# The 48 T sums of the gate and up stage made by GpSimd instead of VectorE

## The chip, the core and the metric

The kernel runs on one core of one Trainium2 chip. The metric is the device time of one execution, in microseconds (us). A core has a TensorE (PE in the profile), a VectorE (DVE), a ScalarE (ACT), a GpSimd (POOL) and a SyncE (SP). Each works through its own instructions in order and waits on semaphores for the others. SyncE and GpSimd also issue the DMA transfers.

## The reference

With x of 2048 tokens by 640, the kernel computes a gated mix of a Fourier layer and a feed-forward layer, all in float32:

```python
g = _sigmoid((x * gate_w).sum(-1, keepdims=True))
a = einsum("ts,bse->bte", seq_re, x @ hid_re.T) - einsum("ts,bse->bte", seq_im, x @ hid_im.T)
b = (_gelu(x @ w_gate) * (x @ w_up)) @ w_down      # 640 -> 1728 -> 640
return g * a + (1 - g) * b
```

The change lies in the middle of `b`: in the inner values `_gelu(x @ w_gate) * (x @ w_up)` and in what is prepared from them for the product with `w_down`.

## The kernel before, in words

**Products.** Every float32 operand is split into a high part (ACT, line 82) and a low part (DVE, line 85: raw minus high), and a product is three matmuls (`mm3`, lines 101 to 103). On top of that the products are made in blocks of two by two with sums of blocks (Strassen and Winograd), so that seven products stand for eight. The sums of blocks of a right operand are called T here, those of the weights S.

**Stages.** In the profiled execution a first stage (to about 54 us) prepares the tokens and makes block 0 of the 1728 inner columns. The gate and up stage (about 54 to 340 us) is the loop over `f` = 1 to 12 at line 1182, 128 inner columns each. After it come the product with `w_down` (loop over `kseq`, line 1269), and then the two Fourier products.

**Inner values.** For each `f` and each half of the tokens, `tp` = 0 or 1, the generator `gate_up` makes two tiles of 128x512, `s2` and `s1` (gelu of the gate times the up product; lines 556, 561 and 563). `keep` (line 398) stores each to DRAM in `hA` by a DMA issued from GpSimd. Two neighbouring `f` make a pair `k`. Per pair and `tp` four T sums of inner values are stored in `hT`: one at the end of the odd `f` (line 566), three after the even `f` (`last_sums`, lines 573 and 575, and `last_sum`, line 579). That is 6 pairs x 2 x 4 = 48 sums. Some of these tiles are reused soon: the buffer `s5` that holds the sums of lines 566 and 575 is one of those that the next blocks take again, as are the buffers of `s2` and `s1`.

**Products across the halves.** In odd blocks from `f` = 3 on, `together` and `together_up` make products whose right operand is a sum over the two token halves, T1 to T3. These three do not fit in on-chip memory all the time: for `f` = 5, 7, 9 and 11 they are loaded again from DRAM by `load_across` (line 1153), 512 KB each, issued from GpSimd: `xq` for `together` late in the even block ahead, `xu` for `together_up` inside the odd block (line 1249). `together_up` needs T1 first, in the product into `pZ..u`.

**What sets the order.** Inside the loop the order of PE, ACT, DVE and GpSimd is the order of the Python code (`in_order`, line 1181). The steps of `gate_up`, `together` and `together_up` follow each other as the loops at lines 1238 to 1248 say. Between them `fill` (line 1158) takes side work from the list `fills`: weight sums and splits for the next block, `make_up` (the S sums and splits of `together_up`'s weights, whose high part is `wu3h` and so on), and the T sums of the pair before, which come from `todo` at line 1187. Each piece has a cost in units that the author chose; `fill` goes on while the cost done is under 1.25 times the share of PE work done, but it ends its turn before a piece of cost 0 once it has done one (line 1162). In blocks 5, 7, 9 and 11 the T sums come first in the list; in block 3 they follow the sums over the halves.

Of the kernel before, what the change touches and what calls it, by code (L numbers as in the profile page):

```python
# [12 lines left out]
ALU = mybir.AluOpType  # L13
# [24 lines left out]
def kernel(  # L38
# [27 lines left out]
    nc = tc.nc  # L66
# [8 lines left out]
    def mtile(dt, name):  # L75
        return pool.tile([P, T], dt, tag="m", name=name, bufs=14)

    def bank(name):
        return psum.tile([P, T], F32, tag="ps", name=name, bufs=8)
# [19 lines left out]
    def mm3(ps, lhs, rhs, first, last):  # L99
        (lh, ll), (rh, rl) = lhs, rhs  # L100
        nc.tensor.matmul(ps, lh, rh, start=first, stop=False, skip_group_check=True)  # L101
        nc.tensor.matmul(ps, lh, rl, start=False, stop=False, skip_group_check=True)  # L102
        nc.tensor.matmul(ps, ll, rh, start=False, stop=last, skip_group_check=True)  # L103
# [32 lines left out]
    def pair(dt, name):  # L136
        return slot(dt, [P, 2, T], name)
# [4 lines left out]
    def at(hilo, i):  # L142
        h, l = hilo
        return h[:, i], l[:, i]

    def copy(src, name):
        m = mtile(F32, name)
        nc.scalar.activation(m, src, AF.Copy)  # L148
        return m

    tt = nc.vector.tensor_tensor
# [53 lines left out]
    def pair_of(f):  # L205


        return 0 if f < PAIRED or f >= NF else 2 - (f - PAIRED + 1) % 2
# [188 lines left out]
    def keep(to, i, src):  # L397
        nc.gpsimd.dma_start(to[:, i], src)  # L398
# [21 lines left out]
    hid, todo = {}, deque()  # L420
# [74 lines left out]
    def gate_up(f, W, B, tp, s5, s1t, xs, s4):  # L495

        n = f"{f}_{tp}"  # L500
        kind = pair_of(f)
        X, Z = bank(f"pX{n}"), bank(f"pZ{n}")
        xs[tp] = X
        x1, x2 = at(B[5], 0), at(B[5], 1)
        k, second = divmod(f - 1, 2)

        def prod(ps, a, b, first):
            for i in range(2):
                mm3(ps, W[a, i], at(B[b], i), first and i == 0, True)

        prod(X, "A11", (1, 1), True)
        yield 136
        if not kind:
            V = bank(f"pV{n}")
            nc.scalar.activation(V, X, AF.Copy)
        else:
            s1 = s1t[kind - 1, tp] if (kind, tp) != (1, 1) else None
            if s1 is not None:
                tt(s1, s1, X, op=ALU.add)
        yield  # L520
        if not kind:
            prod(V, "A12", (2, 1), False)
            mm3(V, W["g5"], x1, False, True)
            yield 204
            s1 = mtile(F32, f"s1{n}")
            nc.scalar.activation(s1, V, AF.Gelu_apprx_tanh)
            yield
        prod(Z, "S1", "T1", True)
        mm3(Z, W["u5"], x2, False, True)
        yield 204  # L530
        nc.scalar.activation(s5, Z, AF.Copy)
        yield
        prod(X, "S2", "T2", False)
        yield 136
        s2 = copy(X, f"s2{n}")
        yield
        mm3(Z, W["D"], x2, False, False)
        yield 68
        if kind:
            s1 = s1t[kind - 1, tp]  # L540
            nc.scalar.activation(s1, s1, AF.Gelu_apprx_tanh)
        yield
        prod(X, "S3", "T3", False)
        yield 136
        tt(s5, s5, X, op=ALU.add)  # L545
        yield
        prod(Z, "S4", (2, 2), False)
        yield 136
        tt(s2, s2, Z, op=ALU.add)  # L549
        nc.scalar.activation(s2, s2, AF.Gelu_apprx_tanh)  # L550
        yield
        if not kind:
            prod(X, "A22", "T4", False)
        mm3(X, W["u5"], x1, False, True)
        yield 68 if kind else 204
        tt(s2, s2, s5, op=ALU.mult)  # L556
        keep(hA[tp][k], 1 + 2 * second, s2)
        if kind:
            c21 = s4[kind - 1, tp]
            tt(c21, c21, X, op=ALU.add)  # L560
            tt(s1, s1, c21, op=ALU.mult)
        else:
            tt(s1, s1, X, op=ALU.mult)
        keep(hA[tp][k], 2 * second, s1)
        if not second:
            tt(s5, s2, s1, op=ALU.subtract)
            keep(hT[tp][k], 0, s5)
            hid[tp] = s2, s5
            yield
        h12, t1 = hid.pop(tp)  # L570

        def last_sums():
            tt(h12, s2, h12, op=ALU.subtract)  # L573
            keep(hT[tp][k], 2, h12)
            tt(t1, s2, t1, op=ALU.subtract)
            keep(hT[tp][k], 1, t1)

        def last_sum():
            tt(s5, s1, t1, op=ALU.subtract)
            keep(hT[tp][k], 3, s5)  # L580

        todo.extend([(122, last_sums), (61, last_sum)])
        yield

    def sums_left(engine, a11, a12, a22, a21, to):
# [595 lines left out]
    with in_order(PE, ACT, DVE, POOL):  # L1181
        for f in range(1, NF):
# [41 lines left out]
            s5 = pair(F32, f"s5{f}")  # L1224
            xs = {}
            work = [gate_up(f, W, Bs[tp], tp, s5[:, tp], s1t, xs, s4) for tp in range(2)]
            more = together(f, W, Tp, s1t, xs) if kind == 1 else iter(())
            more_up = together_up(f, W, up, s4) if kind == 1 else iter(())
# [124 lines left out]
    for i, (j, ri, b, sp) in enumerate(cseq):  # L1353
# [65 lines left out]
        else:  # L1419
# [21 lines left out]
            if lst:  # L1441
                for d in range(2):
                    s2 = copy(X[d], f"s2{n}{d}")
# [10 lines left out]
                for d in range(2):  # L1454
                    s2, a, r, c12 = sv["s2", d], sv["a", d], sv["r", d], sv["c12", d]
# [41 lines left out]
    for i, (tp, b, p) in enumerate(useq[: 3 * ND]):  # L1497
# [43 lines left out]
        for q in range(2):  # L1541
            s2, a = es[q]
            tt(a, s2, Q[q], op=ALU.add)
        for q in range(2):
            s2, a = es[q]
# [47 lines left out]
    for q in range(2):  # L1593
        tail(X[q], ("A11", q, True), 0)
        sv["x", q] = copy(X[q], f"yx{q}")
        s2, c21, c22 = es[q]
# [105 lines left out]
```

## Time and profile before

| | |
|---|---|
| three timed runs | 1020.31, 1021.18 (median), 1022.54 us |
| span of the profiled execution, first to last instruction | 1019.2 us |
| timed runs above that span | 1.1 to 3.3 us, the median 2.0 us |
| busy, whole span | PE 1014.9, DVE 826.7, ACT 485.1, POOL 163.2 us |
| busy from 54 to 340 us (gate and up) | PE 286.00, DVE 228.05, ACT 135.48, POOL 73.67 us |
| granted TensorE clock | 1.000 |

No time of the profiled execution is listed apart from its span, so the span stands for it, and the 2.0 us to the median are what lies around it. A row of a view of groups reads: line, engine, operation, out<-in, shapes, count, then busy us and mean ns of one, then the idle time of the engine ahead of them and what ended it. A row of the timeline reads: start in us from the span's start, length in us, engine, line, operation, and in brackets the engine's idle time ahead of it and who ended it. A DMA row of POOL is the time in which GpSimd issues it; its landing is given apart. A matmul row lasts 0.39 us, but the next one starts about 0.23 us later.

### The profile page before, as it was taken

What the parts mean: (1) busy time and instruction counts of PE and PEld (TensorE: products, weight loads), DVE (VectorE), ACT (ScalarE), POOL (GpSimd) and SP (SyncE); (2) the same over time, 40 slices, a digit from 0 to 9 for tenths busy, and PEclk for the clock granted to TensorE, in tenths of its full rate; (3) what the DMA queues carried; (4) which work ended last, traced back from release to release, by engine and by line L of the source; (5) the groups of instructions that cost most, each with busy time, mean ns of one, the idle gap of its engine ahead of it and who ended that gap; (6) DMA issues with size and microseconds to landing.
All of it is one profiled execution on the core that took longest, in us unless ns stands there. A gap on an engine that the chain in (4) does not pass through costs nothing.

```text
span 1019.2 us, 13255 instructions
## 1 busy us (share of the span) xinstructions
PE 1014.9 (100%) x4483; PEld 840.1 (82%) x4483; DVE 826.7 (81%) x1158; ACT 485.1 (48%) x618; POOL 163.2 (16%) x291
## 2 busy tenths in 40 slices
PE   9999999999999999999999999999999999999998
PEld 7888888888888888888888888888888888888887
DVE  6987887977687979988887976898488859797796
ACT  5544535353535577557444443444344345455440
POOL 0122241323221200100001012102210200021121
PEclk9999999999999999999999999999999999999999
DMA  7468577968689999968874669658866877897855
GB/s 271 168 210 274 182 270 241 311 226 280 200 286 287 407 364 413 355 233 331 295 258 173 209 242 330 218 196 296 296 209 208 300 250 273 292 350 219 273 143 89
DMA packets 96068, 265.74 MB, mean 261 GB/s; under 512 B 12608, under 2 KB 26944, under 8 KB 96000
## 3 DMA queue, kind: packets, MB, share of 16 engines
q1 hardware_dynamic: 70512, 185.24, 52.9%
q0 software_dynamic: 25200, 79.46, 23.1%
q8 instruction: 35, 0.57, 0.2%
q14 instruction: 33, 0.27, 0.1%
q10 hardware_dynamic: 288, 0.20, 0.1%
HBM read 192.48 MB, written 70.27 MB: 258 GB/s over the span
## 4 chain that ended last, share of the span: by engine, by line
PE 100%; DVE 0%; issue 0%
PE pX L102 7%; PE pX L101 7%; PE pX L103 7%; PE pZ L101 5%; PE pZ L102 5%; PE pZ L103 5%; PE pL L103 3%; PE pL L101 3%; PE pL L102 3%; PE pV L103 2%; PE pV L101 2%; PE pV L102 2%; PE pR L103 1%; PE pY L103 1%; PE pQ L103 1%; PE pQ L101 1%
## 5 line engine op out<-in xcount | busy, mean ns | idle before, releaser
L82 ACT ACTIVATE ch<-csa 128x1024 fp32r<-128x1024 f32 x32 | 34.0, 1062 | 78.5 <-DVE csa L764 77.1
L85 DVE TENSOR_TENSOR cl<-cra,ch 128x1024 fp32r<-128x1024 f32 x32 | 39.1, 1222 | 27.0 <-ACT ch L82 24.9
L82 ACT ACTIVATE ch<-cra 128x1024 fp32r<-128x1024 f32 x32 | 33.9, 1059 | 52.3 <-DVE cl L85 16.3
L85 DVE TENSOR_TENSOR cl<-crb,ch 128x1024 fp32r<-128x1024 f32 x32 | 39.1, 1223 | 14.5 <-ACT ch L82 14.5
L103 PE MATMUL pL<-ch,xal 128*128 128x512 f32 x128 | 49.8, 389 | 0.0
L102 PE MATMUL pL<-cl,xah 128*128 128x512 f32 x128 | 49.8, 389 | 0.0
L101 PE MATMUL pL<-ch,xah 128*128 128x512 f32 x128 | 49.7, 389 | 0.0
L398 POOL DMA_DIRECT2D hA<-s x48 | 26.1, 544 | 138.1 <-DVE s L556 118.5
L82 ACT ACTIVATE ch<-crb 128x1024 fp32r<-128x1024 f32 x32 | 33.8, 1055 | 29.7 <-PE pL L102 11.6
L85 DVE TENSOR_TENSOR cl<-csb,ch 128x1024 fp32r<-128x1024 f32 x32 | 39.2, 1225 | 3.7 <-ACT ch L82 2.3
L85 DVE TENSOR_TENSOR cl<-csa,ch 128x1024 fp32r<-128x1024 f32 x32 | 39.1, 1221 | 2.1 <-ACT ch L82 1.1
L82 ACT ACTIVATE ch<-csb 128x1024 fp32r<-128x1024 f32 x32 | 34.0, 1062 | 11.7 <-DVE csb L767 5.0
L550 ACT ACTIVATE s<-s 128x512 f32<-128x512 f32 x24 | 15.2, 633 | 47.6 <-DVE s L549 47.6
L148 ACT ACTIVATE s<-pX 128x512 f32<-128x512 f32 x40 | 23.7, 596 | 29.0 <-PE pX L103 28.4
L82 ACT ACTIVATE kh<-kw 128x1024 fp32r<-128x1024 f32 x24 | 25.3, 1054 | 18.9 <-DMA kw<-wsd 14.5
L85 DVE TENSOR_TENSOR kl<-kw,kh 128x1024 fp32r<-128x1024 f32 x24 | 29.3, 1220 | 4.3 <-ACT kh L82 4.3
L545 DVE TENSOR_TENSOR s<-s,pX 128x512 f32<-128x512 f32 x24 | 16.4, 685 | 19.2 <-PE pX L103 19.1
L1349 POOL DMA_DIRECT2D uA<-c x8 | 4.3, 541 | 168.9 <-DVE c L1451 168.6
L398 POOL DMA_DIRECT2D hT<-s x48 | 26.0, 541 | 18.5 <-DVE s L573 8.1
L923 POOL DMA_DIRECT2D out<-ks x12 | 6.5, 541 | 137.4 <-DVE ks L922 136.5
L102 PEld LDWEIGHTS pL<-cl,xah 128*128 128x128 f32 x128 | 24.0, 188 | 5.0
L103 PEld LDWEIGHTS pL<-ch,xal 128*128 128x128 f32 x128 | 24.0, 188 | 5.0
(3626 smaller groups left out, 3479.0 us busy)
## 6 DMA issues: line engine op xcount, KB each, us to landing
cra<-in_ct SPq DMA_DIRECT2D x64, 512.0 KB, 4.2
crb<-in_ct SPq DMA_DIRECT2D x64, 512.0 KB, 5.0
hA<-s POOLq DMA_DIRECT2D x48, 256.0 KB, 5.7
hT<-s POOLq DMA_DIRECT2D x48, 256.0 KB, 5.0
kr<-hA SPq DMA_DIRECT2D x24, 512.0 KB, 7.7
kr<-hT SPq DMA_DIRECT2D x24, 512.0 KB, 7.3
ux<-uA SPq DMA_DIRECT2D x24, 512.0 KB, 6.2
ux<-uT SPq DMA_DIRECT2D x16, 512.0 KB, 7.3
```

What stands on the lines that cost most here:

```text
L82: nc.scalar.activation(hi, raw, AF.Copy)
L85: nc.vector.tensor_tensor(lo, raw, hi.bitcast(F32), op=ALU.subtract)
L101: nc.tensor.matmul(ps, lh, rh, start=first, stop=False, skip_group_check=True)
L102: nc.tensor.matmul(ps, lh, rl, start=False, stop=False, skip_group_check=True)
L103: nc.tensor.matmul(ps, ll, rh, start=False, stop=last, skip_group_check=True)
L148: nc.scalar.activation(m, src, AF.Copy)
L398: nc.gpsimd.dma_start(to[:, i], src)
L545: tt(s5, s5, X, op=ALU.add)
L550: nc.scalar.activation(s2, s2, AF.Gelu_apprx_tanh)
L923: nc.gpsimd.dma_start(acc4[:, t] if tp and e == 4 else out[2 * tp + t, e], src)
L1349: nc.gpsimd.dma_start(to[:, i], src)
```

## The change

Four `tt(...)`, which is `nc.vector.tensor_tensor`, become `nc.gpsimd.tensor_tensor`, and the costs that `fill` counts for the three late sums go from 122 and 61 to 0:

```diff
         if not second:
-            tt(s5, s2, s1, op=ALU.subtract)
+            nc.gpsimd.tensor_tensor(s5, s2, s1, op=ALU.subtract)
             keep(hT[tp][k], 0, s5)
...
         def last_sums():
-            tt(h12, s2, h12, op=ALU.subtract)
+            nc.gpsimd.tensor_tensor(h12, s2, h12, op=ALU.subtract)
             keep(hT[tp][k], 2, h12)
-            tt(t1, s2, t1, op=ALU.subtract)
+            nc.gpsimd.tensor_tensor(t1, s2, t1, op=ALU.subtract)
             keep(hT[tp][k], 1, t1)
 
         def last_sum():
-            tt(s5, s1, t1, op=ALU.subtract)
+            nc.gpsimd.tensor_tensor(s5, s1, t1, op=ALU.subtract)
             keep(hT[tp][k], 3, s5)
 
-        todo.extend([(122, last_sums), (61, last_sum)])
+        todo.extend([(0, last_sums), (0, last_sum)])
```

The instructions of GpSimd from the end of block 4 into block 5, before. `hA` and `hT` are the stores of inner values and of T sums, `xu` the loads of T1, T2 and T3 for `together_up`:

```order
L398 DMA hA_72<-s_1004 128x512
L398 DMA hT_78<-s_0_1122 128x512
L398 DMA hT_78<-s_985 128x512
L398 DMA hT_78<-s_1257 128x512
L398 DMA hT_84<-s_1_1136 128x512
L398 DMA hT_84<-s_985 128x512
L398 DMA hT_84<-s_1257 128x512
L1153 DMA xu_1485<-xv_562 128x1024
L1153 DMA xu_1527<-xv_563 128x1024
L1153 DMA xu_1529<-xv_564 128x1024
```

The same place on GpSimd in the change, from behind the last store of inner values to ahead of the first `xu` load:

```order
L573 TENSOR_TENSOR s_0_1112<-s_0_1321,s_0_1112 128x512
L398 DMA hT_78<-s_0_1112 128x512
L575 TENSOR_TENSOR s_985<-s_0_1321,s_985 128x512
L398 DMA hT_78<-s_985 128x512
L579 TENSOR_TENSOR s_1257<-s_1102,s_985 128x512
L398 DMA hT_78<-s_1257 128x512
L573 TENSOR_TENSOR s_1_1124<-s_1_1329,s_1_1124 128x512
L398 DMA hT_84<-s_1_1124 128x512
L575 TENSOR_TENSOR s_985<-s_1_1329,s_985 128x512
L398 DMA hT_84<-s_985 128x512
L579 TENSOR_TENSOR s_1257<-s_1004,s_985 128x512
L398 DMA hT_84<-s_1257 128x512
```

Between the last store of inner values and the first `xu` load stood six DMA issues; now six sums and six DMA issues stand there. The places in front of blocks 7, 9 and 11 are alike.

The instructions of ACT in block 3, before. `wu3h` is the high part of `together_up`'s weights, L468 the copy of `pH3u` into the bank `pV3u`, L148 are copies out of a bank:

```order
L148 ACTIVATE s_1110<-pH3t 128x512
L148 ACTIVATE s_0_1122<-pX_0_1026 128x512
L82 ACTIVATE wu3h<-wu3r 128x640
L148 ACTIVATE s_1_1136<-pX_1_1039 128x512
L468 ACTIVATE pV3u<-pH3u 128x512
L541 ACTIVATE s_1017<-s_1017 128x512
```

And in the change:

```order
L148 ACTIVATE s_1102<-pH3t 128x512
L148 ACTIVATE s_0_1112<-pX_0_1024 128x512
L148 ACTIVATE s_1_1124<-pX_1_1035 128x512
L468 ACTIVATE pV3u<-pH3u 128x512
L82 ACTIVATE wu3h<-wu3r 128x640
L541 ACTIVATE s_1017<-s_1017 128x512
```

The four pieces of cost 0 (two with two sums, two with one) take a turn of `fill` each, so the split of `wu3` comes two instructions later on ACT, behind L468. In blocks 5, 7 and 9 a split of a weight sum (`wa6` in block 5) comes earlier on ACT in the same way: it now stands ahead of the copies of `pH5t` and `pX` that come before L468.

The instructions of GpSimd at the end of block 1, before. `hA_65` and `hA_71` are the stores for the two halves of the tokens, `hT_77` and `hT_83` those of the first T sums, and `xp` stands for loads of block 2:

```order
L398 DMA hA_65<-s_0_651 128x512
L398 DMA hA_65<-s_0_606 128x512
L398 DMA hT_77<-s_565 128x512
L398 DMA hA_71<-s_1_664 128x512
L398 DMA hA_71<-s_1_619 128x512
L398 DMA hT_83<-s_565 128x512
L1138 DMA xp_559<-xp_790 128x512 x2
```

And in the change:

```order
L398 DMA hA_65<-s_0_651 128x512
L398 DMA hA_65<-s_0_606 128x512
L566 ISA
L566 TENSOR_TENSOR s_565<-s_0_651,s_0_606 128x512
L398 DMA hT_77<-s_565 128x512
L398 DMA hA_71<-s_1_664 128x512
L398 DMA hA_71<-s_1_619 128x512
L566 TENSOR_TENSOR s_565<-s_1_664,s_1_619 128x512
L398 DMA hT_83<-s_565 128x512
L1138 DMA xp_559<-xp_790 128x512 x2
```

Besides the two sums there is a new instruction, `L566 ISA`, which the build puts ahead of the first sum: it makes GpSimd load its instruction library. The first sum on GpSimd reads a buffer that the sum `xpt` at line 1122 of block 2 takes next on DVE, so that one now waits for GpSimd's sum; and on ACT the split of `xpt` (line 82) stands ahead of the copy at line 515 from bank `pX` into `pV`, on which PE goes on in block 2.

The order of PE does not change in the gate and up stage.

## The prediction

> **What bounds the kernel now.** The page of the profile comes first: its span, its busy shares, and the end of its chain of waits.
>
> ```profile
> span 1019.2 us, 13255 instructions
> PE 1014.9 (100%) x4483; PEld 840.1 (82%) x4483; DVE 826.7 (81%) x1158; ACT 485.1 (48%) x618; POOL 163.2 (16%) x291
> PE 100%; DVE 0%; issue 0%
> ```
>
> Then the view by windows for the gate and up stage (stretch, sum, then busy time of PE, PEld, DVE, ACT, POOL, then the granted clock), and the waits of PE over the whole span:
>
> ```profile
> 54.00:340.00 286.00, 286.00 (x1261) 236.36 (x1260) 228.05 (x414) 135.48 (x213) 73.67 (x133) 1.00 0.77 258
> PE idle L1017 <- PEq L1690: 0.8, 1, 0.8
> ```
>
> PE is busy for 286.00 of 286.00 us at full clock, and waits 0.8 us in all. DVE is busy 228.05 us there and gives up 48 sums, but nothing on PE waits for DVE, so this relief can bring no more than those 0.8 us. Conversely any operand that comes late adds its whole delay to the time, since PE has no pause that could take it up. So the question is which operands come late, and by how much. I went through the program of the change for what PE waits on, and set each against the time in this trace; three places matter.
>
> **What one sum costs.** On DVE the rows by groups are these; the last is the nearest to a slower reader:
>
> ```profile
> L566 DVE TENSOR_TENSOR s<-s,s 128x512 f32<-128x512 f32 x12 | 8.3, 692 | 0.4
> L575 DVE TENSOR_TENSOR s<-s,s 128x512 f32<-128x512 f32 x12 | 8.2, 684 | 0.0
> L85 DVE TENSOR_TENSOR ws6l<-ws6r,ws6h 128x1024 fp32r<-128x1024 f32 x1 | 1.2, 1220 | 0.0
> ```
>
> DVE loses 48 x 0.69 = 33 us, which is worth nothing. No row shows GpSimd computing. Call the duration of one sum on it g. The lower bound is 0.69 (as fast as DVE). The nearest row is 1.22, DVE over 1024 elements: the 512 of the one input and the 512 of the other, taken one after the other. To it I add the chance to meet DVE at the memory: DVE is busy (228.05 - 33) / 286 = 0.68 of the time, and half of its mean instruction there (228.05 / 414 = 0.55) is 0.27, so 0.68 x 0.27 = 0.19. I take g = 1.40 (an estimate), and as upper bound 1.22 + 0.69 = 1.91, where each sum waits for a whole DVE instruction.
>
> The Trainium skill, "GPSIMD Engine Reference", section "Elementwise — side-by-side cycle accounting", gives 4497 ns for a float32 addition over 2048 elements on GpSimd, 1.96 times DVE's, and keeps elementwise work on DVE; a quarter of it is 1.12 us (an estimate from that page). By it the sum below would be 4 x 1.83 + 1.2 + 4.3 = 12.8 instead of 19.8, and the time 1034.0. No trace here shows it yet.
>
> **Blocks 5, 7, 9 and 11: T1 comes late.** GpSimd's timeline in block 5, the same place in block 11, and PE's first use of T1 (tile `xu`) in both:
>
> ```profile
> 147.27 1.14 POOL L398 DMA_DIRECT2D hT<-s  x2
> 148.60 0.54 POOL L398 DMA_DIRECT2D hT<-s  x1 [0.19 <-issue]
> 152.13 0.55 POOL L1153 DMA_DIRECT2D xu<-xv  x1
> 290.31 1.14 POOL L398 DMA_DIRECT2D hT<-s  x2
> ```
>
> ```profile
> 161.26 0.40 PE L101 MATMUL pZ5u<-xu,wu5h 128*128 128x512 f32 x1
> 304.30 0.40 PE L101 MATMUL pZ11u<-xu,wu11h 128*128 128x512 f32 x1
> ```
>
> The landing of that first `xu` load after its issue, in blocks 7, 5 and 11:
>
> ```profile
> DMA to landing us min/median/max: 4.9/4.9/4.9
> DMA to landing us min/median/max: 5.3/5.3/5.3
> DMA to landing us min/median/max: 7.1/7.1/7.1
> ```
>
> From the place of the first `hT` store to PE's first use of T1 there are 161.26 - 147.27 = 13.99 us, in block 11 also 304.30 - 290.31 = 13.99. In the change the first sum starts there, and six sums with six stores stand ahead of the load. Two stores took 1.14, so 0.57 each; with 0.13 for the hand-over (under the 0.19 of "issue" in the second row) one sum and its store take g + 0.70. With the shortest landing, 4.9, since the stores now come less densely, T1 is late by 6 x (g + 0.70) + 4.9 - 13.99 = 3.51 us at g = 1.40. The four blocks are built alike: 4 x 3.51 = 14.0. At g = 1.22 it is 4 x 2.43 = 9.7, at 1.60 4 x 4.71 = 18.8. It is nothing up to g = 0.81. What hid the loads was the 9 us between issue at 152.13 and use; that cover is gone at g = 0.81.
>
> A second path runs beside it. On ACT the split of `wa6` now stands ahead of L468, and its input was computed by DVE into a buffer that a stored sum must leave first:
>
> ```profile
> DMA to landing us min/median/max: 3.9/3.9/3.9
> 159.21 0.62 ACT L82 ACTIVATE wa<-wa6r 128x512 fp32r<-128x512 f32 x1
> 160.83 0.58 ACT L468 ACTIVATE pV5u<-pH5u 128x512 f32<-128x512 f32 x1 [0.15 <-PE pH5u L103]
> 162.66 0.39 PE L101 MATMUL pV5u<-xT04h,wa5h 128*128 128x512 f32 x1
> ```
>
> The sixth store issues at 147.27 + 12.6 - 0.6 = 159.3 and lands 3.9 later, at 163.2; DVE, split, two copies and L468 follow, some 2.6 us in all, so `pV5u` is ready at 165.8. PE, late by 3.51, asks for it at 162.66 + 3.51 = 166.2. It lies beside the first delay and costs nothing more.
>
> **Block 3: a split behind L468.** ACT and PE there:
>
> ```profile
> 111.89 0.74 ACT L82 ACTIVATE wu3h<-wu3r 128x640 fp32r<-128x640 f32 x1 [0.31 <-DVE wu3r L249]
> 113.04 0.58 ACT L468 ACTIVATE pV3u<-pH3u 128x512 f32<-128x512 f32 x1
> 113.53 0.62 ACT L541 ACTIVATE s<-s 128x512 f32<-128x512 f32 x1
> 112.67 0.83 DVE L85 TENSOR_TENSOR wu3l<-wu3r,wu3h 128x640 fp32r<-128x640 f32 x1 [0.81 <-ACT wu3h L82]
> 113.53 0.40 PE L101 MATMUL pZ3u<-xv,wu3h 128*128 128x512 f32 x1
> 114.00 0.40 PE L103 MATMUL pZ3u<-xv,wu3l 128*128 128x512 f32 x1
> ```
>
> The split now starts where L541 did, at 113.53, and ends at 114.27, where PE wants `wu3h` at 113.53: about 0.8 late. The low part starts 0.78 after the split began (112.67 - 111.89) and takes 0.83, so it ends at 115.14, where PE wants it at 114.00: 1.14 late, of which the first 0.8 are the same delay. With the hand-over some 1.2 us in all, once. The sums do not enter here: it follows from the costs set to 0.
>
> **Block 2: the library.** The program of the change has `L566 ISA`, the load of GpSimd's library, ahead of the first sum:
>
> ```profile
> 69.83 0.54 POOL L398 DMA_DIRECT2D hA<-s  x1 [0.89 <-DVE s L563]
> 72.63 0.69 DVE L1122 TENSOR_TENSOR xpt<-xp,xp 128x512 f32<-128x512 f32 x1 [0.43 <-DMA hA<-s]
> 73.41 0.63 ACT L82 ACTIVATE xp<-xpt 128x512 fp32r<-128x512 f32 x1 [0.69 <-DVE xpt L1122]
> 73.94 0.58 ACT L515 ACTIVATE pV<-pX 128x512 f32<-128x512 f32 x1
> 75.34 0.39 PE L101 MATMUL pV<-x121h,wa2h 128*128 128x512 f32 x1
> ```
>
> DVE's L1122 now waits also for the first sum; behind it queue DVE's further sums and splits of `xp`, and on ACT the split of `xpt`, then L515, whose bank PE needs at 75.34. Let R be the load of the library. Load and sum start at 70.4 + 0.2 = 70.6; then come L1122 to the split's start (0.78), the split to L515 (0.53) and L515 to PE (0.6): PE is late by 70.6 + R + g + 1.91 - 75.34 = R + g - 2.83. No row shows R. From below it is 0 (a load that runs ahead of need); another engine's load of tables is the first row here, and transfers that GpSimd issues, the `xu` loads, the second:
>
> ```profile
> L690 ACT ACT_TABLE_LOAD x2 | 2.6, 1283 | 0.0
> DMA to landing us min/median/max: 3.4/6.0/7.5
> ```
>
> I take R = 6.0, the median of that second row, since code must come from DRAM by a transfer, too; the bounds are 0 and 7.5. That makes 6.0 + 1.4 - 2.83 = 4.6 us, once.
>
> The same page, section "Instruction dispatch", says that the first call of freshly loaded code pays about 5.95 us. By it this term would be 5.95 + 1.12 - 2.83 = 4.2.
>
> **The sum.** 14.0 + 1.2 + 4.6 = 19.8; the span becomes 1019.2 + 19.8 = 1039.0, and with the 2.0 us from span to median (1021.18 - 1019.2) 1041.0. The single sums of line 566 in later blocks have nothing tight behind them on GpSimd, and those of block 12 fall into the next stage; I cost both at nothing.
>
> **The rivals.** (1) *Sums that DVE blocks.* g = 1.91: each sum waits for a whole instruction of DVE. For it: DVE is still busy 68% of the time, with sums of two inputs. Then 4 x (6 x 2.61 + 4.9 - 13.99) = 26.3, plus 1.2, plus 6.0 + 1.91 - 2.83 = 5.1: 32.6, or 1053.8. Against it: a third of the time DVE is idle. The skill's "SBUF — State Buffer", section "Who interferes with whom", states this rule: a DVE instruction with two inputs in SBUF and a GpSimd one that reads SBUF exclude each other, and the second waits fully.
>
> (2) *Only what happens once.* g at 0.7 to 0.8, as on DVE: T1 is in time, and 1.2 + 6.0 + 0.7 - 2.83 = 5.1 remain: 1026.3. For it, the 692 ns row, and that GpSimd is busy only 73.67 of 286 us; against it, that nothing else suggests DVE's pace on this engine.
>
> (3) *Not slower.* The point that decides is g up to 0.81 together with R + g up to 2.83, a library loaded within 2 us (as in the ACT row, 1.28). Then all sums hide, only block 3's 1.2 us stays, and the time is 1022.4: no change.
>
> (4) *Faster.* It would need a wait of PE to remove, and the view of waits has 0.8 us of them.
>
> **How the numbers follow.** My forecast has 0.60, with a range of its own from g = 1.22 and R = 4 (9.7 + 1.2 + 2.4 = 13.3, 1034.5) to g = 1.60 and R = 7.5 (18.8 + 1.2 + 6.3 = 26.3, 1047.5). Rival 1 has 0.20, 2 has 0.10, 3 has 0.07 and 4 has 0.03. The range goes from 1027, just above rival 2, to 1056, which takes in rival 1 with R = 7.5 (34.1, 1055.3): 0.20 is left out, all of it below. A measurement of this kernel tells changes from about 0.2%, 2.0 us: faster 0.03, within 0.07, slower 0.90.
>
> **What would show it.** In the new profile PE should wait at `pZ5u`, `pZ7u`, `pZ9u` and `pZ11u` for the `xu` load, 3.5 us each; at `pV` of block 2 for ACT, 4.6 us; at `pZ3u` for `wu3h` and `wu3l`, 1.2 us together. Six pairs of sum and store should take 12.6 us on GpSimd. I am wrong if the rows of sums on GpSimd are under 0.81 or over 1.91 us, if the library shows no gap behind 70 us, or if PE waits at other places: for stores that must leave a buffer, or for DVE behind GpSimd.

## The result, and the profile after

| | before | after |
|---|---|---|
| median | 1020.95 us (4 runs, 1020.31 to 1022.54) | 1055.04 us (4 runs, 1052.01 to 1056.47) |
| span of the profiled execution | 1019.2 us | 1050.2 us |
| PE busy in it | 1014.9 us | 1026.7 us |

The ratio is 1.0328, with a 95% interval of 1.0314 to 1.0342: 3.3% slower, 34 us. The profiled execution of the change is the shortest of its four, 31.0 us above the one of before, so the accounts below come to 31.0.

These are the page's span and busy shares of the change:

```profile
span 1050.2 us, 13255 instructions
PE 1026.7 (98%) x4483; PEld 845.8 (81%) x4483; DVE 843.7 (80%) x1110; ACT 484.1 (46%) x618; POOL 227.7 (22%) x339
```

The 31.0 us fall into two parts. PE's idle time went from 1019.2 - 1014.9 = 4.3 to 1050.2 - 1026.7 = 23.5 us: 19.2 more. And PE's busy time went from 1014.9 to 1026.7 for the same 4483 matmuls: 11.8 more. DVE, which gave up 33 us of sums, is not less busy but more: 843.7 instead of 826.7.

The waits of PE in the change (place, operand waited for, us in all, times, longest):

```profile
PE pH7t L101 <- DVE s L448: 5.2, 1, 5.2
PE pH9t L101 <- DVE s L448: 3.1, 1, 3.1
PE pH11t L101 <- DVE s L448: 3.0, 1, 3.0
PE pH5t L101 <- DVE s L448: 3.0, 1, 3.0
PE kZ L102 <- DVE kb0011l L85: 1.8, 1, 1.8
PE pZ3u L103 <- DVE wu3l L85: 1.0, 1, 1.0
PE idle L1017 <- PEq L1690: 0.8, 1, 0.8
PE pZ11u L101 <- DMA xu<-xv: 0.7, 1, 0.7
PE pZ3u L101 <- ACT wu3h L82: 0.6, 1, 0.6
```

Nothing but the line "idle" was there before. 14.3 us of these waits are at a place that the prediction's terms do not have: `pH5t` to `pH11t`, where PE waits until DVE has read the bank in L448. The wait at `kZ`, with one of 0.4 at `kL`, lies behind the stage, in the product with `w_down`. T1 (`xu`), which was to cost 14.0, costs 0.7.

Why L448 is late is seen on DVE in block 7 (start, length, then the line). L714 multiplies a tile of tokens by `gate_w` and sums it, L246 and L249 are S sums of the weights `wu7`, L85 makes their low part, and L519 and L448 add a bank to a sum:

```profile
205.60 1.84 DVE L714 CUSTOM_DVE_ANT_0 xz<-xz,gwb 128x640 f32<-128x640 f32 x1 [3.35 <-DMA xz<-in_xz]
207.37 1.82 DVE L246 TENSOR_TENSOR wu7r<-wu7r 128x128 f32<-128x128 f32 x1
209.63 1.84 DVE L249 TENSOR_TENSOR wu7r<-wu7r 128x128 f32<-128x128 f32 x1
211.39 0.67 DVE L519 TENSOR_TENSOR s<-s,pX 128x512 f32<-128x512 f32 x1
212.32 1.95 DVE L85 TENSOR_TENSOR wu7l<-wu7r,wu7h 128x640 fp32r<-128x640 f32 x1 [0.26 <-ACT wu7h L82]
214.19 2.34 DVE L714 CUSTOM_DVE_ANT_0 xz<-xz,gwb 128x640 f32<-128x640 f32 x1
216.46 0.68 DVE L448 TENSOR_TENSOR s<-s,pH7t 128x512 f32<-128x512 f32 x1
```

and beside it on GpSimd:

```profile
205.44 1.30 POOL L575 TENSOR_TENSOR s<-s,s 128x512 f32<-128x512 f32 x1
207.73 1.30 POOL L579 TENSOR_TENSOR s<-s,s 128x512 f32<-128x512 f32 x1
210.01 1.30 POOL L573 TENSOR_TENSOR s<-s,s 128x512 f32<-128x512 f32 x1
212.30 1.27 POOL L575 TENSOR_TENSOR s<-s,s 128x512 f32<-128x512 f32 x1
214.56 1.27 POOL L579 TENSOR_TENSOR s<-s,s 128x512 f32<-128x512 f32 x1
```

The same instructions took, in the trace of before (the second L714 0.82 as well):

```profile
198.19 0.82 DVE L714 CUSTOM_DVE_ANT_0 xz<-xz,gwb 128x640 f32<-128x640 f32 x1
199.54 0.28 DVE L246 TENSOR_TENSOR wu7r<-wu7r 128x128 f32<-128x128 f32 x1
200.26 0.29 DVE L249 TENSOR_TENSOR wu7r<-wu7r 128x128 f32<-128x128 f32 x1
201.79 0.82 DVE L85 TENSOR_TENSOR wu7l<-wu7r,wu7h 128x640 fp32r<-128x640 f32 x1
```

Read the starts and ends together. L246 ends at 207.37 + 1.82 = 209.19, the sum beside it at 207.73 + 1.30 = 209.03; L249 ends at 211.47, its sum at 211.31. So both, 0.28 us long by themselves, end 0.16 behind a sum. The other three, 0.82 us long by themselves, end 0.70 behind one: the first L714 at 207.44 and its sum at 206.74, L85 at 214.27 and 213.57, the second L714 at 216.53 and 215.83. Nearly all of the work of each is done only when the sum is over. The five long ones have both inputs in on-chip memory and lose 1.02 + 1.54 + 1.55 + 1.13 + 1.52 = 6.8 us together. L519 and L448, one of whose inputs is a bank that PE wrote (`pX`, `pH7t`), take 0.67 and 0.68 as ever. GpSimd hardly suffers: these sums take 1.27 to 1.30 and none of the stage more than 1.45; behind it three take 1.72 to 1.93.

This is the exclusion that the Trainium skill, "SBUF — State Buffer", section "Who interferes with whom", states for a DVE instruction with two inputs there and a GpSimd instruction that reads there; the trace agrees, and here it is DVE that waits, up to the whole remaining length of a sum.

The second half of it is the order on DVE. Before, L448 stood ahead of the sums for `wu7`; in the change it stands behind them, behind the split `wu7l` and behind a second L714, since the pieces of cost 0 end turns of `fill` and later pieces go to earlier turns. Block 5, whose rows are alike, before and after:

```
before                        after
L714 xz<-xz,gwb               L714 xz<-xz,gwb
L448 s<-s,pH5t                L246 to L249 wu5r<-wu5r
L246 to L249 wu5r<-wu5r       L519 s<-s,pX
L453, L454                    L85 wu5l<-wu5r,wu5h
L85 wu5l<-wu5r,wu5h           L714 xz<-xz,gwb
L714 xz<-xz,gwb               L448 s<-s,pH5t
```

The six sums that left DVE ahead of the first L714 do not bring L448 earlier either. In the four blocks DVE now stands idle there for 2.4 to 3.4 us, 10.8 in all, until the load of `xz` has landed (3.35 in block 7, in the brackets above).

Most of the 11.8 us of longer busy time is in the view by windows (stretch, its length, PE busy with its matmuls, then granted clock) around the pauses; this is block 7's:

```profile
212.00:214.00 2.00, 0.00 (x0) 1.00 0.34 131
214.00:216.00 2.00, 0.00 (x0) 0.76 0.41 82
216.00:218.00 2.00, 0.81 (x2) 0.50 0.95 375
218.00:220.00 2.00, 2.00 (x6) 0.50 0.84 176
220.00:222.00 2.00, 2.00 (x7) 0.54 0.67 221
222.00:224.00 2.00, 2.00 (x10) 1.00 1.03 295
```

The clock is 1.00 when PE stops at 212, falls to 0.50 some 3 us later, and stays there until about 221.5, over 4 us into the work that goes on: 6 to 7 matmuls start in 2 us there, and 10 in the row behind. Summed over all such windows of the run, PE's busy time times the part of the clock that is missing makes some 10 of the 11.8 us (an estimate from these rows). The rest comes with the pauses themselves, as busy time also rises by 1.7 us in the run with copies below, where no window of the stage is under 1.00.

### The profile page after: what moved, and what is told of

The parts are those of the page before. It is cut to its first block, busy times and chain, and to the rows that moved or that the text cites. A ratio compares the mean times of both kernels' runs of the same rounds, so it can differ in the third digit from the quotient of the medians.

```text
span 1050.2 us, 13255 instructions
## 1 busy us (share of the span) xinstructions
PE 1026.7 (98%) x4483; PEld 845.8 (81%) x4483; DVE 843.7 (80%) x1110; ACT 484.1 (46%) x618; POOL 227.7 (22%) x339
## 4 chain that ended last, share of the span: by engine, by line
PE 80%; DVE 4%; DMA 3%; issue 1%; POOL 1%; ACT 0%; POOLq 0%; ACTq 0%; SPq 0%; DVEq 0%
PE pX L101 5%; PE pX L102 5%; PE pX L103 5%; PE pZ L102 3%; PE pZ L101 3%; PE pZ L103 3%; PE pL L102 3%; PE pL L101 3%; PE pL L103 3%; PE pY L102 1%; PE pR L102 1%; PE pV L102 1%; PE pQ L101 1%; PE pY L101 1%; PE pQ L102 1%; PE pV L101 1%
## 5 line engine op out<-in xcount | busy, mean ns | idle before, releaser
L85 DVE TENSOR_TENSOR cl<-cra,ch 128x1024 fp32r<-128x1024 f32 x32 | 39.1, 1222 | 26.2 <-ACT ch L82 24.1
L85 DVE TENSOR_TENSOR cl<-crb,ch 128x1024 fp32r<-128x1024 f32 x32 | 39.1, 1222 | 15.0 <-ACT ch L82 15.0
L85 DVE TENSOR_TENSOR cl<-csb,ch 128x1024 fp32r<-128x1024 f32 x32 | 39.2, 1224 | 3.7 <-ACT ch L82 2.3
L85 DVE TENSOR_TENSOR cl<-csa,ch 128x1024 fp32r<-128x1024 f32 x32 | 39.1, 1221 | 2.1 <-ACT ch L82 1.1
L82 ACT ACTIVATE ch<-csb 128x1024 fp32r<-128x1024 f32 x32 | 34.0, 1062 | 11.8 <-DVE csb L767 4.5
L148 ACT ACTIVATE s<-pX 128x512 f32<-128x512 f32 x40 | 23.7, 596 | 30.2 <-PE pX L103 29.7
L85 DVE TENSOR_TENSOR kl<-kw,kh 128x1024 fp32r<-128x1024 f32 x24 | 31.0, 1291 | 4.4 <-ACT kh L82 4.4
L82 ACT ACTIVATE kh<-kw 128x1024 fp32r<-128x1024 f32 x24 | 25.3, 1053 | 18.4 <-DMA kw<-wsd 8.1
L531 ACT ACTIVATE s<-pZ 128x512 f32<-128x512 f32 x24 | 13.9, 594 | 40.7 <-DMA hT<-s 19.2
L714 DVE CUSTOM_DVE_ANT_0 xz<-xz,gwb 128x640 f32<-128x640 f32 x16 | 20.2, 1261 | 10.8 <-DMA xz<-in_xz 10.8
```

Source lines behind the costliest of these rows:

```text
L82: nc.scalar.activation(hi, raw, AF.Copy)
L85: nc.vector.tensor_tensor(lo, raw, hi.bitcast(F32), op=ALU.subtract)
L714: nc.vector.tensor_tensor_reduce(v, v, gwb, 1.0, 0.0, ALU.mult, ALU.add, z[:, sb : sb + 1])
```

## The experiments

The theory after the result (A): the pauses at `pH5t` to `pH11t` need both halves, the order that puts L448 behind two-input work, and GpSimd's reading sums that hold this work up; T1 is as late as forecast but hidden behind these pauses; and each pause is paid again in part by a halved clock. The rivals are B (the order alone), C (GpSimd's queue or stores, without the exclusion) and D (T1 is not late at all).

**The order alone.** The sums stay on VectorE, the costs are 0.

```diff
-        todo.extend([(122, last_sums), (61, last_sum)])
+        todo.extend([(0, last_sums), (0, last_sum)])
```

> The sums stay on VectorE, but the costs are 0 as in the change, so VectorE and ScalarE get the change's order. Theory A (the pauses at pH5t to pH11t come from GpSimd's sums that hold up VectorE's instructions with two inputs in on-chip memory): none of these pauses, because the work that now stands ahead of L448 takes 4.1 us and not 9.6, and L448 comes at 157.5 (in the time of the change), 1.9 us before TensorE asks. Only the pause in block 3 is left, 1.2 us as forecast (wu3l not held up) and about 1.5 us of halved clock behind it: 1023 to 1025 us. Theory B (the new order alone puts L448 late): pauses of about 3 us at pH5t, pH9t, pH11t and 5 at pH7t stay, 1040 to 1055 us.

Measured: 1023.46 us against 1020.4, ratio 1.0026 (1.0015 to 1.0036). The waits of PE in it, beside the 0.8 of "idle" and one of 0.2 in the first 5 us:

```profile
PE pZ9u L101 <- DMA xu<-xv: 0.7, 1, 0.7
PE pZ3u L101 <- ACT wu3h L82: 0.6, 1, 0.6
```

B falls: with the order of the change, and DVE loaded with all sums besides, no wait at `pH.t` is left; in block 5 L448 ends at 155.43, 1.0 us before PE uses the bank. The total is as A has it; inside it, block 3 costs 0.6 and not 1.2 (only `wu3h` is late), without a lower clock behind it, and T1 is 0.7 late in block 9.

**The sums alone.** GpSimd makes the sums, with the costs of before, so L448 stands ahead of the `wu` sums again.

```diff
-        todo.extend([(0, last_sums), (0, last_sum)])
+        todo.extend([(122, last_sums), (61, last_sum)])
```

> The sums on GpSimd, but with the costs 122 and 61 of before, so L448 stands ahead of the wu sums on VectorE again, and block 3 has its old order. Theory A: the pauses at pH5t to pH11t and at pZ3u are gone, and now the lateness of T1 that they covered comes out: six cycles of 2.28 us are 13.7, plus 4.9 of landing, less 13.99: 4.6 us of waiting at pZ5u, pZ7u, pZ9u, pZ11u (or 4 us at pV5u and its like for L468 behind the split of wa6), and about 2.5 us of halved clock each, so 4 x 7 = 28, 1045 to 1052 us. Theory D (T1 is not late, only the pauses at pH.t matter): 1021 to 1026 us.

Measured: 1054.29 us, ratio 1.0328 (1.0313 to 1.0344), the same time as the change's and above A's range of 1045 to 1052. It comes by other waits; the longest are these:

```profile
PE pZ L101 <- ACT s L531: 5.1, 3, 1.8
PE pZ11u L101 <- DMA xu<-xv: 4.9, 1, 4.9
PE pZ5u L101 <- DMA xu<-xv: 3.6, 1, 3.6
PE pZ9u L101 <- DMA xu<-xv: 3.0, 1, 3.0
PE pZ7u L101 <- DMA xu<-xv: 3.0, 1, 3.0
```

The pauses at `pH.t` are gone, and T1 is 4.9 + 3.6 + 3.0 + 3.0 = 14.5 us late, four times 3.6. That is the prediction's first term (14.0), at its place. D falls. A wait that no theory had named came with it: ACT's L531, the copy out of `pZ`, waits for a stored T sum to leave its buffer, 5.1 us in three pauses. They end about 1 us ahead of T1's place in blocks 5, 7 and 9 and take part of its lateness: both waits together are 5.4, 4.7, 4.7 and 4.9 us in the four blocks, near the 4.6 that the formula gives with cycles of 2.28. Waits of 1.7 at `pH3u` and 2.2 in the product with `w_down` were not in A's sum.

**GpSimd busy without reading.** The change, with three fills in place of each sum (the sums are left out).

```diff
-            nc.gpsimd.tensor_tensor(s5, s2, s1, op=ALU.subtract)
+            for _ in range(3):
+                nc.gpsimd.memset(s5, 0.0)
```

> As the change, but in place of each of the 48 sums GpSimd fills the same tile with zeros three times (so the sums are left out); that writes on-chip memory and reads none of it. Theory A (the hold-up needs a GpSimd instruction that reads on-chip memory): VectorE's split to wu5l takes 0.83 us again and not 1.96, and the pauses at pH5t to pH11t are gone. If three fills take about as long as a sum (1.3 us), T1 is late as forecast for the costs of before, 1045 to 1052 us; if they take under 0.8 us together, only block 3 is left, 1023 to 1026 us. Theory C (any GpSimd instruction of that length holds VectorE up, or the pauses come from late stores): the pauses at pH.t stay, 1045 to 1055 us with wu5l near 2 us or with VectorE waiting for stores.

Measured: 1063.58 us, ratio 1.0421 (1.0405 to 1.0437). Three fills turned out longer than a sum; GpSimd and DVE in block 5:

```profile
158.82 1.71 POOL L578 MEMSET s<- 128x512 f32 x3
161.48 1.71 POOL L583 MEMSET s<- 128x512 f32 x3
```

```profile
154.35 0.83 DVE L85 TENSOR_TENSOR wu5l<-wu5r,wu5h 128x640 fp32r<-128x640 f32 x1 [0.26 <-ACT wu5h L82]
155.84 0.68 DVE L448 TENSOR_TENSOR s<-s,pH5t 128x512 f32<-128x512 f32 x1
```

GpSimd is occupied longer than in the change, in the same order and with the same stores, and yet `wu5l` takes 0.83 and not 1.96 us, and L448 starts at 155.84 instead of 161.61. PE has no wait at `pH.t` of over 0.2. So C falls for these pauses. The wait for `xz` falls as a cause, too: the row of the same L714 (L718 in this kernel) has a longer one than in the change,

```profile
151.73 0.82 DVE L718 CUSTOM_DVE_ANT_0 xz<-xz,gwb 128x640 f32<-128x640 f32 x1 [4.39 <-DMA xz<-in_xz]
```

and L448 follows it after 4.1 us, against 9.6 in the change. The time lies above the ranges of both theories, since the 1045 to 1052 us expected were for fills as long as a sum; with a cycle of 161.48 - 158.82 = 2.66 the prediction's formula gives 6 x 2.66 + 4.9 - 13.99 = 6.9 us of late T1, and the waits at `pZ5u` to `pZ11u` are 7.5, 6.8, 7.5 and 7.3.

**One input instead of two.** The change, with a copy of the first input in place of each sum (the subtraction is left out).

```diff
-            nc.gpsimd.tensor_tensor(s5, s2, s1, op=ALU.subtract)
+            nc.gpsimd.tensor_copy(s5, s2)
```

> As the change, but each sum on GpSimd is a copy of its first input (the subtraction is left out): one input instead of two. Theory A (any GpSimd instruction that reads on-chip memory holds VectorE's two-input instructions up): wu5l on VectorE again takes over 1.2 us, as long as the copy runs, and not 0.83. If the copy takes 0.7 to 0.9 us, a cycle is 1.7 to 1.9, T1 is late by at most 2 us and the pauses at pH.t are under 2 us: 1024 to 1038 us; if it takes 1.3 us like the sum, 1050 to 1056 us. Rival (it takes two inputs on GpSimd to hold VectorE up): wu5l takes 0.83 us and there is no pause at pH.t.

Measured: 1028.49 us, ratio 1.0077 (1.0062 to 1.0092). GpSimd's copies take 0.63 to 0.71 us on the mean. DVE in block 5:

```profile
154.35 1.24 DVE L85 TENSOR_TENSOR wu5l<-wu5r,wu5h 128x640 fp32r<-128x640 f32 x1 [0.26 <-ACT wu5h L82]
```

and the longest of PE's four equal waits at `pH.t`:

```profile
PE pH11t L101 <- DVE s L448: 1.0, 1, 1.0
```

A copy holds DVE up as well: in block 5 it takes 0.62 us, and the five instructions are 0.41 to 0.84 us longer than in the trace of before. L448 is late by 1.0 us in each of the four blocks, and T1 is in time. The rival, that it takes two inputs, falls.

**The loads of T1 on another queue.** Once with the change and once with the costs of before:

```diff
-        nc.gpsimd.dma_start(v.bitcast(F32), kept[k - 1])
+        (nc.sync if n == "xu" else nc.gpsimd).dma_start(v.bitcast(F32), kept[k - 1])
```

> As the change, but the loads of T1, T2 and T3 for together_up are issued by SyncE, so they no longer stand behind GpSimd's sums. Theory A (in the change the lateness of T1 runs beside the pauses at pH5t to pH11t and adds almost nothing to them): the four pauses at pH.t stay at 3 to 5 us, the 0.7 us at pZ11u goes, and the time is 1050 to 1056 us, as the change within 0.5%. Rival (late T1 loads, or their traffic, are part of what makes the change slow): under 1045 us.

Measured: 1053.82 us, ratio 1.0324 (1.0300 to 1.0347), the change's time. The four pauses at `pH.t` stay at 5.2, 3.0, 3.0 and 3.0, and no wait for T1 is left. So in the change T1's lateness lay beside them. The next path behind also shows: PE waits 3.0 us at `pV9u` for ACT's L468. L468 stands there on ACT behind the split of `wa10`; the prediction had this path, in block 5 with `wa6`, as one that lies beside T1.

> Sums on GpSimd, costs 122 and 61 of before, loads of T1 to T3 issued by SyncE: both long waits are taken away. Theory A: no waits at pH.t and at pZ.u; left are L531 behind the landing of a stored T sum (5.1 us in three pauses with the old costs alone), the product with w_down at 1.8 + 0.4, pH3u at 1.7, and L468 behind the split of wa6 by up to 1 us in each of four blocks; with some halved clock 1029 to 1040 us. Rival (the sums on GpSimd cost nothing once L448 and T1 are in time): 1020 to 1024 us.

Measured: 1037.21 us, ratio 1.0156 (1.0139 to 1.0173): within A's range, but only in part by the waits that it named. L531 is no longer among them; loads of T2 or T3, at `pH5u`, `pH7u` and `pH9u`, are new with 5.9 us. What is left includes, beside the same 1.8 at `kZ`,

```profile
PE pH5u L101 <- DMA xu<-xv: 2.2, 1, 2.2
PE pH3u L101 <- ACT s L148: 1.7, 1, 1.7
```

With both long waits taken away about half of the loss is gone, and the rest is spread over small ones: these `xu` loads, L468 (0.3 to 0.7 in four blocks), the stage after. No one cause for this rest was isolated.

**The early sums alone.** The kernel before, with only the 12 sums of line 566 on GpSimd.

```diff
-            tt(s5, s2, s1, op=ALU.subtract)
+            nc.gpsimd.tensor_tensor(s5, s2, s1, op=ALU.subtract)
```

> The kernel before with the 12 sums of line 566 alone on GpSimd; the 36 late ones stay on VectorE with their old costs, so the order is that of before. Theory A: no T1 load and no L448 stands behind these sums, GpSimd's library takes no time (the change showed 0.04 us), and TensorE has no new pause of over 1 us: 1020 to 1023 us. Rival (VectorE held up by any GpSimd sum costs TensorE, wherever it stands): 1025 us and more.

Measured: 1020.59 us against 1020.73, ratio 0.9998 (0.9988 to 1.0007): no change. PE's only wait is the 0.8 of "idle". The library and the hold-ups cost nothing where nothing that PE needs soon stands behind the sums. It also shows the limit from the other side: 12 sums fewer on DVE bring nothing.

**Pauses without GpSimd.** The kernel before, with idle DVE work ahead of L448.

```diff
+        for _ in range({5: 8, 7: 10, 9: 12, 11: 14}.get(f, 0)):
+            tt(s1[1, 1], s1[1, 1], s1[1, 1], op=ALU.max)
         tt(s1[1, 1], s1[1, 1], H, op=ALU.add)
```

> The kernel before, with 8, 10, 12 and 14 idle VectorE instructions (a tile's maximum with itself, 0.60 us apart) ahead of L448 in blocks 5, 7, 9 and 11; GpSimd computes nothing. L448 has 3.83 us to spare there, so TensorE should pause at pH5t, pH7t, pH9t, pH11t for 1.0, 2.2, 3.4 and 4.6 us, 11.2 together. Theory A (the clock falls to half for some microseconds behind any such pause): 1.5 to 3 us more behind each, in all 1038 to 1043 us, with rows of granted clock near 0.5 behind each pause. Rival (the lower clock in the change has to do with GpSimd's work): clock 1.00 throughout and 1032 us.

Measured: 1043.97 us, ratio 1.0228 (1.0211 to 1.0245), 1 us above A's range. The waits of PE (L450 is L448 in this kernel):

```profile
PE pH11t L101 <- DVE s L450: 6.3, 1, 6.3
PE pH9t L101 <- DVE s L450: 4.8, 1, 4.8
PE pH7t L101 <- DVE s L450: 3.4, 1, 3.4
PE pH5t L101 <- DVE s L450: 1.9, 1, 1.9
```

The pauses are longer than expected (the steps between them are 1.4 to 1.5 us for two instructions, 0.72 apiece instead of 0.60) and make 16.4 us. The span grew by 1044.3 - 1019.2 = 25.1, and PE's busy time by 1023.6 - 1014.9 = 8.7: the pauses were paid half again. Windows around the one of block 7:

```profile
208.00:210.00 2.00, 0.00 (x0) 0.81 0.65 164
210.00:212.00 2.00, 1.78 (x4) 0.50 0.45 180
212.00:214.00 2.00, 2.00 (x6) 0.50 0.00 0
```

The same fall to 0.50 without any work on GpSimd: the clock follows PE's pause. From the shift of `pZ..u` less the pause, it cost some 1.9, 3.0, 2.6 and 1.7 us behind the pauses of 1.9, 3.4, 4.8 and 6.3: a longer pause does not cost more here, as in its windows part of the slow stretch passes while PE stands still.

## Why the prediction was right or wrong

The direction held, and 1055.04 lies just inside the range (1027 to 1056), but by luck: the mechanism that made most of the loss is not among the three places of the prediction. The likeliest time, 1041.0, was 14 us too low. Two of the prediction's own signs of being wrong came true: the library shows no gap, and PE waits for DVE behind GpSimd. Step by step:

- **What bounds the kernel** held. Work taken off DVE brought nothing (the early sums alone: 0.9998), and PE's waits went into the time in full, with a lower clock on top.
- **g** was sized well: 1.30 us measured against 1.40, with 0.69 and 1.91 as bounds. Sum and store take 2.28 a cycle against g + 0.70 = 2.10, as the hand-over from sum to store is 0.41 and not 0.13. The 0.19 added for meeting DVE was a wrong step that cost little: in this stage a sum hardly waits for DVE. The Trainium skill's figure (a quarter of 4497 ns, 1.12 us) is 0.18 below the measurement.
- **T1 late, 14.0 us**: right in mechanism, wrong about the change. With the sums alone it is 14.5, and that this is so near is chance: with cycles of 2.28 the formula gives 4 x 4.6 = 18.4, of which pauses at L531 took part ahead of T1. In the change the pauses at `pH.t`, a few microseconds earlier in the same blocks, and the slow clock behind them hold PE back by about as much, and 0.7 is left. The forecast failed in taking it for the first wait of these blocks.
- **"Three places matter"** is the step that failed. Two things were left out. The order on DVE was not gone through as that on GpSimd and ACT was, so that L448 behind the `wu` sums was missed; and where DVE work was timed, it was by the rows of before, as if GpSimd's sums left them alone. Neither alone would have put a wait at `pH.t`: with the order alone there is none, and the sums alone leave L448 in time. Together they make 14.3 us.
- **Block 3, 1.2 us**: 0.6 + 1.0 = 1.6 in the change. By the order alone it is 0.6; the rest is `wu3l`, held up by a sum (1.70 instead of 0.83 us).
- **The library, 4.6 us**: nothing; PE has no wait in block 2. GpSimd's queue shows for it

```profile
L566 POOLq MODIFY_POOL_CONFIG  x2: 37/37/37, 69.5 to 69.6; - x2
```

  and the first sum starts at 69.62, 0.09 after the issue of the store ahead ended. So R is under 0.1, near its lower bound. The 5.95 us of the Trainium skill, "GPSIMD Engine Reference", section "Instruction dispatch", do not appear for this instruction.
- **Rival 1** had the exclusion, but the wrong way round: it let GpSimd wait for DVE. That its 1053.8 lies beside the result is chance; its mechanism would show as sums of 1.9 us, and 1.3 is the median.
- **The sum.** 19.8 us of waits were forecast and 19.2 occurred, which is chance as well: a missed term of 14.3 stands where T1's 14.0 and the library's 4.6 were. What the sum lacked altogether was PE's longer busy time, 11.8 us, most of it by the clock, and the waits in the product with `w_down`, 1.8 + 0.4, where the prediction costed block 12's sums at nothing. `kb0011l`, for which PE waits there, is held up by such a sum as well: 2.29 us, where `kb0010l`, of the same shape, takes 1.21.

The later runs of the change, up to 1056.47, have no trace shown here; that the clock does not fall behind every pause (below) would fit their spread, and was not tested.

## What to carry to other kernels

On a kernel whose bound engine never waits, moving work off another engine has nothing to win, and the question is what stands behind the moved work: go through the order of every engine, and time it with the durations that hold once the moved work runs beside it. GpSimd's reads are not free for VectorE: its two-input work in on-chip memory waited here for up to a whole sum, so such sums belong where no bank or operand that TensorE needs soon stands behind that work. Count a pause of some microseconds of TensorE at about one and a half times its length (31.0 us for 19.2 in the change, 25.1 for 16.4 with DVE work alone), and when one wait is removed, look for the next behind it: without the pauses at `pH.t`, or without T1's lateness, the time stayed as it was.

## What the runs showed of the hardware that was not expected

- The granted clock can fall to 0.50 behind a pause of 1.9 us, and stays there for some microseconds of work. The length of the pause does not decide it. Single pauses of 0.6 and 1.0 us were without it, but in block 3 of the change one of 0.6 and one of 1.0 us stand close together, and the clock fell behind them; behind the same two waits in the run with the change and T1's loads on SyncE it did not. The first row is of the change, the second of that run:

```profile
117.00:118.00 1.00, 1.00 (x4) 0.50 0.08 29
117.00:119.00 2.00, 2.00 (x10) 1.00 0.33 125
```

  Longer pauses can be without it as well: in that run those of 3.0 us in block 9 and in block 11 left the clock at 1.00. Block 11's pause ends in this row:

```profile
323.00:325.00 2.00, 1.03 (x5) 1.00 0.32 131
```

  The Trainium skill, "TensorE: Matmul & The Clock Gate", section "What's actually happening", has a free-running window of about 3.4 us behind this, so that it matters where in the window a pause falls; that would explain all of these, but no run here moved a pause against the window.
- On GpSimd a sum of 128x512 takes 1.30 us, a copy 0.63 to 0.71, a fill 0.53; a store of the result is issued 0.41 us after it, against 0.13 estimated.
- A DVE instruction held up by GpSimd is shown as busy, not as waiting: DVE's busy time went up by 17 us while 33 us of work left it.
